# A feed-forward network moved from behind top-k attention into it, with transposes gathered before one copy

## The chip, the cores and the metric

The kernel runs on one core of a Trainium2 chip. The core has a matrix engine (TensorE, PE), a vector engine (VectorE, DVE), a scalar engine (ScalarE, ACT), GpSimd (POOL) and a queue that issues transfers (SyncE, SP). Every engine works through its own instructions in the order in which the program lists them; semaphores tie the engines together. The metric is the time of the launch on the device in microseconds. The program is written in a tile framework that orders the instructions of each engine when it is built, by its own estimate of when each can start; so the order on an engine isn't always the order of the source.

## The reference, cut to what matters

```python
# q, k, v: (8 batches, 8 heads, 576 positions, 64), f32
scores = scale * np.matmul(q, k.transpose(0, 1, 3, 2))        # 576 x 576 for each head
kth = np.partition(scores, -32, axis=-1)[..., -32:-31]        # the 32nd largest of each row
scores = np.where(scores >= kth, scores, -1e9)                # keep the top 32
attn = np.exp(scores - scores.max(-1, keepdims=True))
attn = attn / (attn.sum(-1, keepdims=True) + 1e-09)
x = np.matmul(attn, v)                                        # then heads side by side:
x = x.transpose(0, 2, 1, 3).reshape(4608, 512)                # 4608 tokens of 512
h = np.maximum(x @ w_in, 0.0)                                 # 512 -> 2048
out = (h * h) @ w_out                                         # 2048 -> 512
```

There are two stages: attention with a top-32 selection in every row, for 64 pairs of batch and head, and then a feed-forward network (FFN) over all 4608 tokens. A token's input to the FFN gathers all eight heads of its batch. So a token can go through the FFN once the eight heads of its own batch are done; it needn't wait for the other batches.

## The kernel before

A head's 576 queries are taken in five tiles: four of 128 rows and one of 64. The top 32 of a row are found by VectorE in four rounds: the eight largest values (`max`), and then their replacement by a very small number (`match_replace`).

```python
    psum_pool = tc.alloc_tile_pool(name="apsum", bufs=2, space=bass.MemoryType.PSUM)
    ...
    def _load_transpose(b, h):            # q, k, v of a head; q and k transposed by TensorE
        ...
        nc.vector.tensor_copy(v_sb[:, :, :], v_sb32[:, :, :])             # L81
        nc.vector.tensor_copy(v_sb2[:, :], v_sb232[:, :])                 # L82
        for c in range(nSK_hi):                                           # four chunks
            tps = psum_pool.tile([128, 128], f32, tag="tps")
            nc.tensor.transpose(tps[:64, :128], q_raw[:128, c, :], id128f[:128, :128])
            nc.scalar.activation(qT[:64, c*128:(c+1)*128], tps[:64, :128], Copy)   # L88
            ...                                                           # the same for k, L91
        ...                                                               # the last 64 of q, k

    def _scores(qT, kT, sq0, ql):
        p0 = psum_pool.tile([128, 512], f32, tag="p0", bufs=1)
        nc.tensor.matmul(out=p0[:ql, :512], lhsT=qT[...], rhs=kT[:64, :512])       # L103
        nc.scalar.activation(scores[:ql, :512], p0[:ql, :512], Copy, scale=scale)  # L104
        p0b = psum_pool.tile([128, 64], f32, tag="p0b", bufs=1)
        ...                                                               # columns 512 to 575

    def _softmax(scores, ql):
        ...                                          # 4 rounds of max and match_replace
        nc.vector.tensor_sub(diff[:ql, :], scores[:ql, :], sc_copy[:ql, :])        # L125
        nc.scalar.activation(attnf[:ql, :], diff[:ql, :], Exp,                     # L128
                             bias=bias_t[:ql, :], accum_out=ssum[:ql, :])
        nc.vector.reciprocal(rsum[:ql, :], ssum[:ql, :])                           # L131
        nc.scalar.activation(attn[:ql, :], attnf[:ql, :], Copy, scale=rsum[:ql, :])

    def _ov(attn, v_sb, v_sb2, b, h, sq0, ql):       # attn transposed, times v
        ov_ps = psum_pool.tile([64, 128], f32, tag="ov")
        for c in range(nSK_hi):
            attnT_ps = psum_pool.tile([128, 128], bf16, tag="attnT")
            attnT_sb = work_pool.tile([128, 128], bf16, tag="attnT_sb")
            nc.tensor.transpose(attnT_ps[:128, :ql], attn[:ql, c*128:(c+1)*128], ...)   # L141
            nc.scalar.activation(attnT_sb[:128, :ql], attnT_ps[:128, :ql], Copy)        # L143
            nc.tensor.matmul(out=ov_ps[:64, :ql], lhsT=v_sb[:128, c, :],                # L144
                             rhs=attnT_sb[:128, :ql], start=(c == 0), stop=False)
        ...                                          # the last 64 columns, L148 to L150
        nc.scalar.activation(ov_sb[:64, :ql], ov_ps[:64, :ql], Copy)                    # L153
        nc.sync.dma_start(out=x_dram[h*64:(h+1)*64, b*S+sq0:b*S+sq0+ql], in_=ov_sb[:64, :ql])

    for b in range(B):
        for h in range(H):
            ...                                      # the five tiles of a head
    # pools of attention released; only then the FFN's pools, weights and loop:
    nc.sync.dma_start(out=w_in_sb32[:, :, :], in_=...)          # 4 MB each, f32
    nc.sync.dma_start(out=w_out_sb32[:, :, :], in_=...)
    nc.vector.tensor_copy(w_in_sb[:, :, :], w_in_sb32[:, :, :])           # L184
    nc.vector.tensor_copy(w_out_sb[:, :, :], w_out_sb32[:, :, :])         # L185
    for mi in range(nMT):                            # nine groups of 512 tokens
        nc.sync.dma_start(out=xT[:, :, :], in_=x_re[:, :, m0:m0+MT])
        for dc in range(nDFF):                       # 16 blocks of the inner width
            for kh in range(KH):                     # 4 matmuls
                nc.tensor.matmul(out=hp[:, :], ...)                       # L203
            nc.scalar.activation(rl[:, :], hp[:, :], Relu)                # L206
            nc.vector.tensor_mul(h2[:, dc, :], rl[:, :], rl[:, :])        # L207
        for mt in range(MT // 128):                  # 4 outputs of 16 matmuls
            ...                                                           # L211
            nc.vector.tensor_copy(osb[:, :], op[:, :])                    # L214
            nc.sync.dma_start(out=out[...], in_=osb[:, :])
```

The attention stage uses eight PSUM banks: two each for `tps`, `attnT` and `ov`, one each for `p0` and `p0b`.

Of the kernel before, what the change touches and what calls it, by code (L numbers as in the profile page):

```python
# [15 lines left out]
def kernel(  # L16
# [49 lines left out]
    def _load_transpose(b, h):  # L66
# [18 lines left out]
        for c in range(nSK_hi):  # L85
            tps = psum_pool.tile([128, 128], f32, tag="tps")
            nc.tensor.transpose(tps[:64, :128], q_raw[:128, c, :], id128f[:128, :128])  # L87
            nc.scalar.activation(qT[:64, c*128:(c+1)*128], tps[:64, :128], Copy)  # L88
            tps = psum_pool.tile([128, 128], f32, tag="tps")
            nc.tensor.transpose(tps[:64, :128], k_raw[:128, c, :], id128f[:128, :128])  # L90
            nc.scalar.activation(kT[:64, c*128:(c+1)*128], tps[:64, :128], Copy)  # L91
        tps = psum_pool.tile([128, 128], f32, tag="tps")
        nc.tensor.transpose(tps[:64, :64], q_raw2[:64, :], id128f[:64, :64])
        nc.scalar.activation(qT[:64, 512:576], tps[:64, :64], Copy)
        tps = psum_pool.tile([128, 128], f32, tag="tps")
        nc.tensor.transpose(tps[:64, :64], k_raw2[:64, :], id128f[:64, :64])
        nc.scalar.activation(kT[:64, 512:576], tps[:64, :64], Copy)
        return qT, kT, v_sb, v_sb2

    def _scores(qT, kT, sq0, ql):  # L100
# [4 lines left out]
        p0b = psum_pool.tile([128, 64], f32, tag="p0b", bufs=1)  # L105
# [30 lines left out]
    def _ov(attn, v_sb, v_sb2, b, h, sq0, ql):  # L136
        ov_ps = psum_pool.tile([64, 128], f32, tag="ov")
        for c in range(nSK_hi):
            attnT_ps = psum_pool.tile([128, 128], bf16, tag="attnT")
            attnT_sb = work_pool.tile([128, 128], bf16, tag="attnT_sb")  # L140
            nc.tensor.transpose(attnT_ps[:128, :ql], attn[:ql, c*128:(c+1)*128],  # L141
                                id128[:ql, :ql])
            nc.scalar.activation(attnT_sb[:128, :ql], attnT_ps[:128, :ql], Copy)  # L143
            nc.tensor.matmul(out=ov_ps[:64, :ql], lhsT=v_sb[:128, c, :],  # L144
                             rhs=attnT_sb[:128, :ql], start=(c == 0), stop=False)
        attnT_ps = psum_pool.tile([128, 128], bf16, tag="attnT")
        attnT_sb = work_pool.tile([128, 128], bf16, tag="attnT_sb")
        nc.tensor.transpose(attnT_ps[:64, :ql], attn[:ql, 512:576], id128[:ql, :ql])  # L148
        nc.scalar.activation(attnT_sb[:64, :ql], attnT_ps[:64, :ql], Copy)  # L149
        nc.tensor.matmul(out=ov_ps[:64, :ql], lhsT=v_sb2[:64, :],  # L150
                         rhs=attnT_sb[:64, :ql], start=False, stop=True)
# [4 lines left out]

    for b in range(B):
        for h in range(H):
            qT, kT, v_sb, v_sb2 = _load_transpose(b, h)
            for (sq0, ql) in qtiles:  # L160
                scores = _scores(qT, kT, sq0, ql)
                attn = _softmax(scores, ql)
                _ov(attn, v_sb, v_sb2, b, h, sq0, ql)

    out_pool.release()
# [5 lines left out]

    KH = d_model // 128
    KHO = d_ff // 128
    DFFC = 128
    nDFF = d_ff // DFFC

    wpool = ctx.enter_context(tc.tile_pool(name="wpool", bufs=1))
    w_in_sb32 = wpool.tile([128, KH, d_ff], f32)
    w_out_sb32 = wpool.tile([128, KHO, d_model], f32)
    nc.sync.dma_start(out=w_in_sb32[:, :, :], in_=moe_w_in.rearrange("(kh p) n -> p kh n", p=128))  # L180
    nc.sync.dma_start(out=w_out_sb32[:, :, :], in_=moe_w_out.rearrange("(kh p) n -> p kh n", p=128))
    w_in_sb = wpool.tile([128, KH, d_ff], bf16)
    w_out_sb = wpool.tile([128, KHO, d_model], bf16)
# [62 lines left out]
```

## Time and profile before

| what | value |
|---|---|
| time, median of 4 runs | 2520.69 us (2519.59 to 2521.15) |
| span of the profiled execution | 2517.8 us |
| TensorE clock granted | 1.00 throughout |
| `max` and `match_replace`, 1280 of each | 0.74 to 0.75 us each |
| copies of `attnT` (ACT, 128 columns) | 1024, 0.276 us each |
| copies of `scores` (ACT, 512 columns) | 320, 0.578 us each |
| Relu of 512 columns (ACT) | 144, 0.597 us each |
| squaring of 512 columns (DVE) | 144, 0.692 us each |
| transfers | 57.24 MB, 23 GB/s on average |

A profile shows one execution. Busy time is the time in which an engine works on an instruction; records of neighbouring instructions on one engine overlap a little, so a group's mean times its count is more than the time it takes. In the lists of waits a line names an engine and what it waited to do, what released it, the sum in us, how often, and the longest. In a timeline a line has the start and the duration in us, the engine (PEld is a weight load of TensorE, SPq a transfer's issue), the source line, the operation and its output and input; in brackets stand the idle time before it and what ended that.

### The profile page before, as it was taken

To read this page: it belongs to the slowest core of one execution; us is meant where nothing else is said; L and a number is where in the kernel's file an instruction comes from. 1 tells how busy PE (TensorE), PEld (TensorE's weight loads), DVE (VectorE), ACT (ScalarE), POOL (GpSimd) and SP (SyncE) were. 2 spreads that over 40 slices of the span, in tenths; PEclk is the share of its full clock that TensorE was granted. 3 is DMA by queue.
4 is the path that set the end of the run, shared out by engine and by line. 5 is a ranking of instruction groups with operands and counts; after the bars stand their busy time and mean duration, and the time that the engine had idled before them with its cause. 6 is when DMAs were issued, how large, how long until landed. Compare 5 with 4: busy or idle time off the path is not lost.

```text
span 2517.8 us, 25279 instructions
## 1 busy us (share of the span) xinstructions
PE 1875.3 (74%) x6272; PEld 832.8 (33%) x6272; DVE 2227.2 (88%) x5110; ACT 1362.9 (54%) x4305; POOL 1.1 (0%) x8
## 2 busy tenths in 40 slices
PE   6777777777777777777777777777777777649999
PEld 3333333333333333333333333333333333314444
DVE  7999999999999999999999999999999999965544
ACT  4555555555555555555555555555555555533333
POOL 0000000000000000000000000000000000000000
PEclk9999999999999999999999999999999999999999
DMA  1000100001000000000000000000000000031111
GB/s 37 16 15 17 25 13 16 15 17 25 12 17 15 17 17 12 16 15 17 17 12 17 15 17 17 14 15 16 15 17 15 15 16 10 3 135 51 53 65 42
DMA packets 155011, 57.24 MB, mean 23 GB/s; under 512 B 143088, under 2 KB 147696, under 8 KB 154352
## 3 DMA queue, kind: packets, MB, share of 16 engines
q1 hardware_dynamic: 154864, 55.62, 8.5%
q8 instruction: 50, 0.82, 0.1%
q14 instruction: 97, 0.79, 0.1%
HBM read 41.42 MB, written 14.16 MB: 22 GB/s over the span
## 4 chain that ended last, share of the span: by engine, by line
DVE 64%; PE 26%; ACT 7%; issue 2%; DMA 1%; SPq 0%; DVEq 0%; ACTq 0%
DVE sc_copy L118 23%; DVE max L117 20%; DVE sc_copy L114 7%; DVE max L113 7%; PE p L103 5%; DVE diff L125 5%; PE op L211 5%; PE hp L203 5%; ACT attnf L128 4%; PE tps L90 2%; PE ov_ps L144 2%; PE attnT_ps L141 2%; PE tps L87 2%; ACT scores L104 1%; DVE rsum L131 1%
## 5 line engine op out<-in xcount | busy, mean ns | idle before, releaser
L103 PE MATMUL p<-kT,qT 64*128 64x512 f32 (+1 forms) x640 | 655.9, 1127 | 508.9 <-ACT scores L104 508.9
L118 DVE MATCH_REPLACE8 sc_copy<-max,sc_copy 128x576 f32<-128x576 f32 (+1 forms) x960 | 713.3, 743 | 0.0
L117 DVE MAX8 max<-sc_copy 128x8 f32<-128x576 f32 (+1 forms) x960 | 711.8, 753 | 0.3
L143 ACT ACTIVATE attnT_sb<-attnT_ps 128x128 bf16<-128x128 bf16 (+1 forms) x1280 | 306.7, 265 | 612.2 <-PE attnT_ps L141 603.2
L144 PE MATMUL ov_ps<-attnT_sb,v_sb 128*64 128x128 bf16 (+1 forms) x1280 | 359.8, 286 | 21.9 <-ACT attnT_sb L143 4.2
L103 PEld LDWEIGHTS p<-kT,qT 64*128 64x128 f32 (+1 forms) x640 | 145.8, 287 | 638.9 <-ACT scores L104 638.0
L128 ACT ACTIVATE attnf<-diff,bias_t 128x576 f32<-128x576 f32 (+1 forms) x320 | 246.8, 771 | 125.0 <-DVE diff L125 125.0
L141 PE MATMUL attnT_ps<-id,attn 128*128 128x128 bf16 (+1 forms) x1280 | 297.9, 283 | 8.8 <-ACT attn L133 8.8
L133 ACT ACTIVATE attn<-attnf,rsum 128x576 bf16<-128x576 f32 (+1 forms) x320 | 248.2, 776 | 29.9 <-DVE rsum L131 13.5
L141 PEld LDWEIGHTS <-attn 128*128 128x128 bf16 (+1 forms) x1280 | 118.2, 110 | 367.6 <-issue 156.0
L125 DVE TENSOR_TENSOR diff<-scores,sc_copy 128x576 f32<-128x576 f32 (+1 forms) x320 | 239.6, 749 | 0.0
L113 DVE MAX8 max<-scores 128x8 f32<-128x576 f32 (+1 forms) x320 | 237.6, 742 | 1.6 <-ACT scores L107 1.5
L114 DVE MATCH_REPLACE8 sc_copy<-max,scores 128x576 f32<-128x576 f32 (+1 forms) x320 | 237.6, 743 | 0.0
L106 PEld LDWEIGHTS p0b<-kT,qT 64*128 64x128 f32 (+1 forms) x640 | 169.6, 300 | 173.4 <-issue 138.3
L144 PEld LDWEIGHTS <-v_sb 128*64 128x64 bf16 x1280 | 171.8, 138 | 144.9 <-issue 58.0
L106 PE MATMUL p0b<-kT,qT 64*128 64x64 f32 (+1 forms) x640 | 190.2, 399 | 0.0
L104 ACT ACTIVATE scores<-p 128x512 f32<-128x512 f32 (+1 forms) x320 | 185.1, 578 | 3.3 <-PE p L103 3.3
L206 ACT ACTIVATE rl<-hp 128x512 f32<-128x512 f32 x144 | 86.0, 597 | 174.2 <-PE hp L203 169.4
L131 DVE RECIPROCAL rsum<-ssum 128x1 f32<-128x1 f32 (+1 forms) x320 | 48.6, 152 | 123.9 <-ACT attnf L128 123.9
L203 PE MATMUL hp<-xT,w_in_sb 128*128 128x512 bf16 x576 | 128.1, 384 | 20.2 <-DVE w_in_sb L184 20.2
L150 PE MATMUL ov_ps<-attnT_sb,v_sb 64*64 64x128 bf16 (+1 forms) x320 | 83.1, 260 | 62.5 <-ACT attnT_sb L149 51.6
L207 DVE TENSOR_TENSOR h<-rl 128x512 bf16<-128x512 f32 x144 | 99.5, 692 | 33.1 <-ACT rl L206 33.0
(39 smaller groups left out, 1445.8 us busy)
## 6 DMA issues: line engine op xcount, KB each, us to landing
out_dram<-osb SPq DMA_DIRECT2D x36, 256.0 KB, 2.0
q_raw<-in_q_dram SPq DMA_DIRECT2D x64, 128.0 KB, 2.2
k_raw<-in_k_dram SPq DMA_DIRECT2D x64, 128.0 KB, 2.4
v_sb<-in_v_dram SPq DMA_DIRECT2D x64, 128.0 KB, 2.2
xT<-attn_x SPq DMA_DIRECT2D x9, 512.0 KB, 3.8
attn_x<-ov_sb SPq DMA_DIRECT2D x256, 16.0 KB, 1.7
w_in_sb<-in_moe_w_in_dram SPq DMA_DIRECT2D x1, 4096.0 KB, 12.7
w_out_sb<-in_moe_w_out_dram SPq DMA_DIRECT2D x1, 4096.0 KB, 23.3
```

What stands on the lines that cost most here:

```text
L103: nc.tensor.matmul(out=p0[:ql, :512], lhsT=qT[:64, sq0:sq0+ql], rhs=kT[:64, :512])
L106: nc.tensor.matmul(out=p0b[:ql, :64], lhsT=qT[:64, sq0:sq0+ql], rhs=kT[:64, 512:576])
L113: nc.vector.max(out=max8[:ql, :], in_=scores[:ql, :])
L114: nc.vector.match_replace(out=sc_copy[:ql, :], in_to_replace=max8[:ql, :], in_values=scores[:ql, :], imm_value=NEG)
L117: nc.vector.max(out=max8[:ql, :], in_=sc_copy[:ql, :])
L118: nc.vector.match_replace(out=sc_copy[:ql, :], in_to_replace=max8[:ql, :], in_values=sc_copy[:ql, :], imm_value=NEG)
L125: nc.vector.tensor_sub(diff[:ql, :], scores[:ql, :], sc_copy[:ql, :])
L128: nc.scalar.activation(attnf[:ql, :], diff[:ql, :], Exp, bias=bias_t[:ql, :], accum_out=ssum[:ql, :])
L141: nc.tensor.transpose(attnT_ps[:128, :ql], attn[:ql, c*128:(c+1)*128], id128[:ql, :ql])
L143: nc.scalar.activation(attnT_sb[:128, :ql], attnT_ps[:128, :ql], Copy)
L144: nc.tensor.matmul(out=ov_ps[:64, :ql], lhsT=v_sb[:128, c, :], rhs=attnT_sb[:128, :ql], start=(c == 0), stop=False)
L203: nc.tensor.matmul(out=hp[:, :], lhsT=w_in_sb[:, kh, dc*DFFC:(dc+1)*DFFC], rhs=xT[:, kh, :], start=(kh == 0), stop=(kh == KH - 1))
```

## The change

The change has two parts. First, transposes are gathered: TensorE writes the transposed chunks side by side into one PSUM bank, and ScalarE copies them out at once instead of one by one. That is done for q and k (four chunks of a head) and for the attention weights (four chunks of a tile; the fifth chunk, of 64 rows, has its own copy). `p0b` shares the two banks of `tps`, and `ov` has one bank instead of two. This leaves two of the eight banks for the FFN.

Second, the FFN becomes a generator that is advanced one piece after each attention tile: the load of a group of tokens, then 16 pieces of four matmuls with Relu and squaring, then a piece of 16 matmuls for each 128 tokens of output. A group is handed out once the batches that hold its tokens have been emitted; groups have 512 tokens, or 128 where fewer are left. The weights are loaded before the third head. What is left after the last batch is done at the end. It is meant to give the engines FFN work while attention runs.

```diff
-        for c in range(nSK_hi):
-            tps = psum_pool.tile([128, 128], f32, tag="tps")
-            nc.tensor.transpose(tps[:64, :128], q_raw[:128, c, :], id128f[:128, :128])
-            nc.scalar.activation(qT[:64, c*128:(c+1)*128], tps[:64, :128], Copy)
-            ...                                                    (k alike, then the last 64)
+        for raw, raw2, dst in ((q_raw, q_raw2, qT), (k_raw, k_raw2, kT)):
+            tps = psum_pool.tile([128, 512], f32, tag="tps")
+            for c in range(nSK_hi):
+                nc.tensor.transpose(tps[:64, c*128:(c+1)*128], raw[:128, c, :], id128f[:128, :128])
+            nc.scalar.activation(dst[:64, :512], tps[:64, :512], Copy)
+            tps = psum_pool.tile([128, 512], f32, tag="tps")
+            nc.tensor.transpose(tps[:64, :64], raw2[:64, :], id128f[:64, :64])
+            nc.scalar.activation(dst[:64, 512:576], tps[:64, :64], Copy)
 ...
-        p0b = psum_pool.tile([128, 64], f32, tag="p0b", bufs=1)
+        p0b = psum_pool.tile([128, 512], f32, tag="tps")
 ...
-        ov_ps = psum_pool.tile([64, 128], f32, tag="ov")
+        ov_ps = psum_pool.tile([64, 128], f32, tag="ov", bufs=1)
+        attnT_ps = psum_pool.tile([128, 5, 128], bf16, tag="attnT")
+        attnT_sb = work_pool.tile([128, 5, 128], bf16, tag="attnT_sb")
         for c in range(nSK_hi):
-            ...                                      (transpose, copy and matmul for each chunk)
+            nc.tensor.transpose(attnT_ps[:128, c, :ql], attn[:ql, c*128:(c+1)*128], id128[:ql, :ql])
+        nc.tensor.transpose(attnT_ps[:64, 4, :ql], attn[:ql, 512:576], id128[:ql, :ql])
+        nc.scalar.activation(attnT_sb[:128, :4, :ql], attnT_ps[:128, :4, :ql], Copy)
+        nc.scalar.activation(attnT_sb[:64, 4, :ql], attnT_ps[:64, 4, :ql], Copy)
+        for c in range(nSK_hi):
+            nc.tensor.matmul(out=ov_ps[:64, :ql], lhsT=v_sb[:128, c, :],
+                             rhs=attnT_sb[:128, c, :ql], start=(c == 0), stop=False)
 ...
+    def _ffn(m0, mt):
+        xT = xpool.tile([128, KH, 512], bf16, tag="xT")
+        nc.sync.dma_start(out=xT[:, :, :mt], in_=x_re[:, :, m0:m0+mt])
+        yield
+        h2 = hpool.tile([128, nDFF, 512], bf16, tag="h2")
+        for dc in range(nDFF):
+            hp = psum_pool.tile([128, 512], f32, tag="ffn", bufs=2)
+            ...                                      (4 matmuls, Relu, squaring, of mt columns)
+            yield
+        for done in range(0, mt, 128):
+            op = psum_pool.tile([128, 512], f32, tag="ffn", bufs=2)
+            ...                                      (16 matmuls, copy, store)
+            yield
 ...
     for b in range(B):
         for h in range(H):
+            if b == 0 and h == 2:
+                ...                                  (the loads and casts of w_in and w_out)
             qT, kT, v_sb, v_sb2 = _load_transpose(b, h)
             for (sq0, ql) in qtiles:
                 scores = _scores(qT, kT, sq0, ql)
                 attn = _softmax(scores, ql)
                 _ov(attn, v_sb, v_sb2, b, h, sq0, ql)
-
+                n_tile += 1
+                if n_tile % 40 != 2:
+                    _piece()                         (advance the FFN by one piece)
+        while given + 128 <= (b + 1) * S:
+            mt = 512 if given + 512 <= (b + 1) * S else 128
+            ready.append(_ffn(given, mt))
+            given += mt
+    while ready:
+        _piece()
-    ...                                              (the FFN's own stage behind attention)
```

## The prediction

> **What bounds the kernel now.** I read the page's busy shares first, then the busy times by stretch, then the waits of VectorE, then the timeline of one head boundary, and last the groups of instructions for durations.
>
> ```profile
> PE 1875.3 (74%) x6272; PEld 832.8 (33%) x6272; DVE 2227.2 (88%) x5110; ACT 1362.9 (54%) x4305; POOL 1.1 (0%) x8
> ```
>
> VectorE (DVE) leads with 88%, but the average mixes two stages. The next view cuts the span at 2240.3 us, where the last attention matmul starts, and at 2260.7 us, where the first FFN matmul starts (columns: stretch, length, busy us and count of each engine, clock, DMA share, GB/s).
>
> ```profile
> 0.00:2240.30 2240.30, 1623.97 (x5120) 719.60 (x5120) 2094.09 (x4928) 1276.63 (x4160) 1.09 (x8) 1.00 0.07 16
> 2240.30:2260.70 20.40, 0.17 (x1) 0.00 (x0) 4.43 (x1) 0.22 (x1) 0.00 (x0) 1.00 0.85 326
> 2260.70:2517.80 257.10, 251.16 (x1152) 113.16 (x1152) 128.70 (x181) 86.04 (x144) 0.00 (x0) 1.00 0.17 59
> ```
>
> So: 2240 us of attention, bound by VectorE (2094 busy, 93%), with TensorE at 72%; 20 us in which the chip only fetches weights; 257 us of FFN, bound by TensorE (251 busy) with VectorE half idle. The limits differ, and the second stage's 277 us are serial behind the first. What VectorE waits for:
>
> ```profile
> DVE rsum L131 <- ACT attnf L128: 123.9, 65, 2.0
> DVE w_in_sb L184 <- DMA w_in_sb<-in_moe_w_in_dram: 18.9, 1, 18.9
> DVE v_sb L81 <- DMA v_sb<-in_v_dram: 8.4, 2, 5.5
> ```
>
> In attention it waits once per head, 65 times, 1.9 us each, for Exp. Why Exp is late is in the timeline of a boundary:
>
> ```profile
> 1005.59 0.75 DVE L125 TENSOR_TENSOR diff<-scores,sc_copy 128x576 f32<-128x576 f32 x1
> ...
> 1008.60 0.27 ACT L91 ACTIVATE kT<-tps 64x128 f32<-64x128 f32 x1
> 1008.85 0.22 ACT L94 ACTIVATE qT<-tps 64x64 f32<-64x64 f32 x1
> ...
> 1008.97 0.76 ACT L128 ACTIVATE attnf<-diff,bias_t 128x576 f32<-128x576 f32 x1
> ...
> 1009.86 0.16 DVE L131 RECIPROCAL rsum<-ssum 128x1 f32<-128x1 f32 x1 [1.99 <-ACT attnf L128]
> ```
>
> Exp's input was ready at 1006.34, and Exp starts at 1008.97: ScalarE (ACT) works in order and stands in a ping-pong of ten small q/k copies with as many transposes, with the attnT copies between them.
>
> **What the Trainium skill says.** "Perfetto Trace Analysis", section Optimization Strategy: where the most contended engine changes over time, interleave the regimes. That is this case, by the second fence. The same page, Optimizing Scalar/DVE Operations: every ScalarE and VectorE operation carries a fixed overhead, of which the record shows about twice what holds the engine, since the write's acknowledgement overlaps with the next operation; grouping into larger operations helps. The trace agrees on the overlap: 0.66 us after the start of a 749 ns subtraction the next operation starts, so 0.09 us are hidden. "ScalarE: Activation LUTs", What ACT_TABLE_LOAD costs, gives 0.833 ns per element; here 64 columns take 223 ns and 128 take 276, 0.83 per element. "TensorE: Matmul & The Clock Gate", Back-to-back issue gap, has about 216 ns for a warm 512-column matmul; the trace has 64 in 13.98 us, 218 ns.
>
> **The change, part by part.**
>
> *Merged copies.* Per head, ten q/k copies (8 x 0.270 + 0.219 + 0.213 = 2.59 us) become four: the 64x512 f32 evacuation takes 0.578 (scores row), so 2 x 0.578 + 2 x 0.216 = 1.59. Saved 1.0 x 64 = 64 us of ScalarE. Per query tile, 4 x 0.276 + 0.269 = 1.37 becomes one copy of 512 columns, estimated at 0.276 + 384 x 0.00083 = 0.595, plus 0.269 = 0.86; saved 0.51 x 320 = 163. None of this is on the bound, but the ping-pong goes.
>
> *Does the 124 us wait go?* I follow one tile in the compiled instruction order of the changed kernel, where Exp(i) starts at 0, with durations from the steady tiles: scores evacuation 0.77, the f32 score matmul 1.40 to 3.4, the five attnT transposes at 0.11 us pace to 4.2, their copies to 5.0, the five output matmuls to 5.7, their copy, and Exp(i+1) can start near 5.9. VectorE asks for it every 2094 / 320 = 6.54 us. It also leaves two 0.66 us operations between the subtraction and the reciprocal, where Exp and its accumulator read need 0.97, so Exp may be 0.35 late for nothing. Ordinary tiles don't stall. With an FFN group of 4 x 0.218 = 0.87 us ahead of the output matmuls the chain takes 6.4, but the tile then has a further 0.6 us VectorE operation: 7.15. At head boundaries there are two orders. In 26 of them (mostly without FFN work beside) the q/k copies are spread over the preceding tile and Exp comes in time. In 37 of them q64, k512, k64 stand ahead of Exp: the chain becomes about 7.6 without and 8.2 with FFN work, where 6.54 + 0.35 and 7.15 + 0.35 + 0.6 are free. That makes 0 to 0.7 us; I take 0.3 x 37 = 11 us. So of 124 us some 110 go.
>
> *Weights early.* The two loads are issued near 8 us, behind the inputs of two heads; they landed 12.7 and 23.3 us after issue in the kernel before, so by 21 and 32. The casts stand in VectorE's order near 23 and 38 us. The 20.4 us go; 8.85 us of casts enter VectorE's stage.
>
> *FFN inside attention.* 4608 tokens become 8 groups of 512 and 4 of 128. All but the last 512 and the last 128 run beside the next batch. They bring to VectorE 7 x 16 = 112 squarings of 512 columns (0.692 alone, 0.60 back to back: 67 us), 48 of 128 columns (estimated 0.692 - 384 x 0.00104 = 0.29, so 0.20: 10 us), 31 output copies (0.60: 19 us), and the casts: 105 us. TensorE gets about 7/8 of 251, some 225 us, so about 1850 in 2240: near 83%, not the bound. The output groups of 16 matmuls (3.5 us) are laid in the compiled order around the output matmuls of a tile; counted as above they end at about 8.4, just before the score matmul that can start at 7.15 + 1.40 = 8.55, and a score block is made almost a tile ahead.
>
> *Batch starts.* In the order, the first relu of a batch stands ahead of the second Exp after the last needed store (store 1.7, load 3.8, four matmuls, relu): about 1.4 us late, 7 times: 10 us.
>
> *Tail.* After the last reciprocal only the last 512 and 128 tokens are left: the fourth tile's store lands and the load of 512 tokens arrives at about +5.5; 16 groups at 0.88 = 14.1; 4 output groups of 16 x 0.218 = 13.9; 16 groups for 128 tokens with two PSUM buffers and relu behind each, estimated 0.5 each = 8; one output group 3.5, copy 0.7, store 2.4, and 0.8 of latencies: 49 us.
>
> *Sum.* VectorE in attention 2094 + 105 inserted + 9 at the start + 9 of small unlisted gaps (2237.3 at the last reciprocal, less 2094 and 134 of listed waits) + 11 + 10 + 1.4 at the last tile = 2239; + 49 tail = 2288; + 3 from span to measured time (2520.7 against 2517.8) = 2291. I say 2295, since what I can have missed is nearly all on the long side.
>
> **The rivals.**
> 1. *The Exp wait stays or moves to every tile.* For it: the boundary chain still has ACT, PE, ACT in turn, and the margin in ordinary tiles is only 0.6 + 0.35 us; FFN matmuls and relus enter both queues in order. Against it: the chain above, and ScalarE falls to about half busy. A stall of 1.9 us per head would give 2295 + 110 = about 2405; 0.3 us on each of 320 tiles about 2390.
> 2. *TensorE becomes the bound in tiles with an output group.* For it: 5.1 us of attention matmul (1624 / 320) plus 3.5 is above 7.15. Against it: busy time counts latency, and score blocks are made ahead. At 2 us for each of 31 groups: 2355.
> 3. *The FFN is hidden entirely and attention stalls vanish.* Then VectorE's work alone counts: about 2270.
> 4. *The FFN stands still while a load is awaited, and VectorE with it,* because queues are in order: each batch would pay a round trip of some 6 us, 7 times: 2330.
>
> **Range and chances.** Rivals 2 to 4 give 2270 to 2355, and rival 1 in full is unlikely, so 2265 to 2350 should hold it 8 times in 10. To miss 2% (2470) nearly all that is hidden would have to come back: chances 94 in 100 faster, 5 within 2%, 1 slower.
>
> **What would show it.** In the changed profile: VectorE busy near 2230 us and above 95%; its wait of reciprocal for Exp below 40 us in all; no long stretch without TensorE before the FFN; ScalarE near 1145 us; last reciprocal near 2240 us; a tail of 45 to 55 us with TensorE full. Wrong would be: a new wait of VectorE for relu (squaring) or for an output group above 30 us; a wait of scores for the score matmul on most tiles; a tail over 60 us.

## The result, and the profile after

| what | before | after |
|---|---|---|
| time, median | 2520.23 us (2519.59 to 2522.05, 13 runs) | 2341.05 us (2337.70 to 2342.45, 8 runs) |
| ratio, with its 95% interval | 1 | 0.9285 (0.9276 to 0.9294) |
| start of the last reciprocal of the attention | 2237.2 us | 2292.0 us |
| from there to the end of the span | 280.6 us | 47.3 us |

The change saves 179 us. The prediction said 2295 us, with 2265 to 2350 as its range; the time is 46 us above the point. The FFN's stage behind the attention is gone as foreseen (280.6 us became 47.3), but the attention grew by 55 us where almost nothing was expected.

The profile after, in the same order as before. The page's busy times, and its TensorE clock in forty slices:

```profile
PE 1758.6 (75%) x6464; PEld 797.6 (34%) x6464; DVE 2199.4 (94%) x5158; ACT 1158.6 (50%) x3009; POOL 1.1 (0%) x8
...
PEclk9999966555566565665656655566555655657558
```

VectorE is at 94% of the span; above 95% was foretold. The busy times by stretch, cut at the last reciprocal (columns as before):

```profile
0.00:2292.20 2292.20, 1720.04 (x6246) 778.40 (x6246) 2180.72 (x5121) 1143.48 (x2973) 1.09 (x8) 0.63 0.09 24
2292.20:2339.30 47.10, 38.60 (x218) 19.17 (x218) 18.67 (x37) 15.12 (x36) 0.00 (x0) 0.92 0.13 43
```

VectorE works 2181 of the first 2292 us, so about 111 us of it are idle. Its list of waits names nearly all of them:

```profile
DVE rsum L126 <- ACT attnf L123: 81.1, 80, 2.4
DVE h L179 <- ACT rl L178: 20.1, 31, 7.1
DVE osb L187 <- PE op L184: 13.3, 5, 2.9
DVE max L108 <- ACT scores L102: 8.5, 21, 0.5
DVE v_sb L81 <- DMA v_sb<-in_v_dram: 8.4, 2, 5.5
```

The wait for the weights is gone. The waits for output groups (`osb`) and 12 of the 20 us for Relu lie in the tail. What remains is the wait of the reciprocal for Exp: 81 us, where the prediction had 12. It is the old wait of 124 us, by the same pair of instructions. All but some 1 us after the last tile lies in batches 1 to 7, 10 to 13 us in each; batch 0, which has no FFN work beside it, has none. And it lies at head boundaries, that is where the next head's q and k are transposed during a head's later tiles. The timeline of one boundary shows why Exp is late:

```profile
799.20 0.47 PE L101 MATMUL p0b<-kT,qT 64*64 64x64 f32 x2
...
807.57 0.59 ACT L89 ACTIVATE qT<-tps 64x512 f32<-64x512 f32 x1
...
808.61 0.31 PE L91 MATMUL tps<-id128f,q_raw 64*64 64x64 f32 x1
...
808.72 0.75 DVE L120 TENSOR_TENSOR diff<-scores,sc_copy 128x576 f32<-128x576 f32 x1
808.96 0.22 ACT L92 ACTIVATE qT<-tps 64x64 f32<-64x64 f32 x1
...
809.23 1.06 PE L88 MATMUL tps<-id128f,k_raw 128*64 128x128 f32 x4 [0.31 <-ACT qT L92]
...
810.33 0.59 ACT L89 ACTIVATE kT<-tps 64x512 f32<-64x512 f32 x1 [1.15 <-PE tps L88]
...
810.97 0.31 PE L91 MATMUL tps<-id128f,k_raw 64*64 64x64 f32 x1 [0.68 <-ACT kT L89]
...
811.32 0.22 ACT L92 ACTIVATE kT<-tps 64x64 f32<-64x64 f32 x1 [0.40 <-PE tps L91]
811.44 0.77 ACT L123 ACTIVATE attnf<-diff,bias_t 128x576 f32<-128x576 f32 x1
...
812.33 0.16 DVE L126 RECIPROCAL rsum<-ssum 128x1 f32<-128x1 f32 x1 [1.27 <-ACT attnf L123]
...
812.68 0.21 ACT L102 ACTIVATE scores<-p0b 64x64 f32<-64x64 f32 x1
```

Exp's input is ready near 809.5, but Exp starts at 811.44. Between them ScalarE, which works in order, waits for k's transposes, and these wait for a bank: the transposes of k start at 809.23, released by the copy of q's last 64 columns, and k's last 64 wait in turn for the copy of its first 512. There are two `tps` banks, but the other one holds `p0b` of the current head's fifth tile since 799.20 (q and k are the next head's), and the copy that frees it (812.68) stands behind Exp. So q64, k512 and k64 take turns in one bank.

The second thing to read is TensorE's pace, here at the first FFN work (start and duration in us):

```profile
278.80 2.07 PE L98 MATMUL p<-kT,qT 64*128 64x512 f32 x2 [0.61 <-ACT scores L99]
...
292.40 3.59 PE L175 MATMUL hp<-xT,w_in_sb 128*128 128x512 bf16 x8
295.92 1.12 PE L98 MATMUL p<-kT,qT 64*128 64x512 f32 x2
```

The same pair of score matmuls takes 2.07 us in one line and 1.12 in the other, 17 us later. The eight FFN matmuls took 3.59 us, 0.449 each; the prediction had 0.218, from a stage in which TensorE ran without a break. So in attention the array mostly runs at half rate, and the clock row agrees from the sixth slice on.

### The profile page after: what moved, and what is told of

It reads as the page before. It is cut to its first block, busy times and chain, and to the rows that moved or that the text cites. A ratio compares the mean times of both kernels' runs of the same rounds, so it can differ in the third digit from the quotient of the medians.

```text
span 2339.3 us, 23300 instructions
## 1 busy us (share of the span) xinstructions
PE 1758.6 (75%) x6464; PEld 797.6 (34%) x6464; DVE 2199.4 (94%) x5158; ACT 1158.6 (50%) x3009; POOL 1.1 (0%) x8
## 4 chain that ended last, share of the span: by engine, by line
DVE 54%; PE 31%; ACT 12%; DMA 2%; issue 2%; SPq 0%
DVE sc_copy L113 18%; DVE max L112 16%; PE p L98 10%; DVE sc_copy L109 6%; DVE max L108 5%; ACT attnf L123 5%; PE hp L175 5%; DVE diff L120 5%; PE tps L88 3%; PE ov_ps L142 3%; PE op L184 3%; PE attnT_ps L136 2%; ACT scores L99 2%; PE p0b L101 2%; DVE h L179 1%
## 5 line engine op out<-in xcount | busy, mean ns | idle before, releaser
L98 PE MATMUL p<-kT,qT 64*128 64x512 f32 (+1 forms) x640 | 609.6, 1051 | 379.6 <-ACT scores L99 379.1
L139 ACT ACTIVATE attnT_sb<-attnT_ps 128x512 bf16<-128x512 bf16 (+1 forms) x320 | 177.5, 555 | 573.1 <-PE attnT_ps L138 572.7
L175 PE MATMUL hp<-xT,w_in_sb 128*128 128x512 bf16 (+1 forms) x768 | 260.0, 459 | 21.0 <-DMA xT<-attn_x 11.2
L147 ACT ACTIVATE ov_sb<-ov_ps 64x128 bf16<-64x128 f32 (+1 forms) x320 | 83.5, 261 | 281.0 <-PE ov_ps L144 280.5
L142 PE MATMUL ov_ps<-attnT_sb,v_sb 128*64 128x128 bf16 (+1 forms) x1280 | 176.2, 286 | 55.5 <-ACT attnT_sb L139 52.8
L136 PE MATMUL attnT_ps<-id,attn 128*128 128x128 bf16 (+1 forms) x1280 | 174.9, 285 | 43.4 <-ACT attn L128 43.2
L101 PEld LDWEIGHTS p0b<-kT,qT 64*128 64x128 f32 (+1 forms) x640 | 146.5, 275 | 158.8 <-ACT attn L128 65.4
L184 PE MATMUL op<-w_out_sb,h 128*128 128x512 bf16 x576 | 180.7, 457 | 21.3 <-DVE h L179 21.1
L142 PEld LDWEIGHTS <-v_sb 128*64 128x64 bf16 x1280 | 125.0, 150 | 177.4 <-issue 156.0
L126 DVE RECIPROCAL rsum<-ssum 128x1 f32<-128x1 f32 (+1 forms) x320 | 50.1, 157 | 81.9 <-ACT attnf L123 81.1
L179 DVE TENSOR_TENSOR h<-rl 128x512 bf16<-128x512 f32 (+1 forms) x192 | 105.8, 554 | 20.1 <-ACT rl L178 20.1
```

Of the source, the lines that this page charges most:

```text
L98: nc.tensor.matmul(out=p0[:ql, :512], lhsT=qT[:64, sq0:sq0+ql], rhs=kT[:64, :512])
L101: nc.tensor.matmul(out=p0b[:ql, :64], lhsT=qT[:64, sq0:sq0+ql], rhs=kT[:64, 512:576])
L136: nc.tensor.transpose(attnT_ps[:128, c, :ql], attn[:ql, c*128:(c+1)*128], id128[:ql, :ql])
L175: nc.tensor.matmul(out=hp[:, :mt], lhsT=w_in_sb[:, kh, dc*DFFC:(dc+1)*DFFC], rhs=xT[:, kh, :mt], start=(kh == 0), stop=(kh == KH - 1))
L184: nc.tensor.matmul(out=op[:, :], lhsT=h2[:, kh, done:done+128], rhs=w_out_sb[:, kh, :], start=(kh == 0), stop=(kh == KHO - 1))
```

## The experiments

Two theories for the 81 us, and both can hold:

- **A, the bank:** `p0b` in the `tps` banks makes q's and k's transposes take turns ahead of Exp.
- **B, the rate:** an FFN group in the attention stage holds TensorE about 1.8 us (4 x 0.449), not 0.87, and so delays what Exp and the scores wait for.

All runs below were timed beside the kernel before, which took 2520 us each time.

### Each theory by itself: e1_own_bank and e2_quarter

e1 gives `p0b` a bank of its own, taken from `attnT`:

```diff
-        p0b = psum_pool.tile([128, 512], f32, tag="tps")
+        p0b = psum_pool.tile([128, 64], f32, tag="p0b", bufs=1)
-        attnT_ps = psum_pool.tile([128, 5, 128], bf16, tag="attnT")
+        attnT_ps = psum_pool.tile([128, 5, 128], bf16, tag="attnT", bufs=1)
```

> The changed kernel, but p0b has a bank of its own again and attnT has one bank in place of two (eight banks as before). In the changed kernel VectorE waits 81 us for Exp, all at head boundaries. Theory A (bank): these come from p0b sharing the two banks of tps: the next tile's p0b holds one bank until its copy, which stands behind Exp, so q64, k512 and k64 take turns in the other bank, transpose and copy one after the other, ahead of Exp. Then the wait falls below 35 us and the time to 2285 to 2305 us. Theory B (rate): they come from FFN matmuls that run at about half the rate that I reckoned with (0.45 to 0.5 us each in place of 0.218) and stand among the boundary's transposes. Then the wait stays above 60 us and the time above 2320 us.

e2 leaves out three of the four products of each `hp` block and twelve of the sixteen of each output; its output isn't the FFN's:

```diff
-            for kh in range(KH):                     # 4
+            for kh in range(1):
-            for kh in range(KHO):                    # 16
+            for kh in range(4):
```

> The changed kernel with a quarter of the FFN's matmuls: one of the four of each hp group and four of the sixteen of each output group; the rest of the products is left out, and all copies, Relus, squarings, loads and stores stay. Theory A (bank): the wait of VectorE for Exp stays above 55 us, and the time falls only by what the tail's matmuls took (some 25 us of 47) plus a little, to about 2305 us. Theory B (rate): the wait falls below 35 us, and the time to about 2265 us.

| run | time | ratio | wait of the reciprocal for Exp | last reciprocal |
|---|---|---|---|---|
| after | 2341.05 us | 0.9285 (0.9276 to 0.9294) | 81.1 us, 80 times | 2292.0 us |
| e1_own_bank | 2299.11 us | 0.9120 (0.9107 to 0.9134) | 55.8 us, 64 times | 2251.1 us |
| e2_quarter | 2293.66 us | 0.9099 (0.9084 to 0.9115) | 56.8 us, 63 times | 2258.5 us |

Each takes a third of the wait away, and neither takes it all. e1 gains 42 us. Only 25 of them are the wait for Exp; VectorE also waits 6 us less for Relu and 5 less for scores in the attention, and works 4 less. e2 gains 47, of which 14 are in the tail, where fewer matmuls are left (33.7 instead of 47.3 us). The same boundary in the timeline of e1:

```profile
774.46 1.06 PE L88 MATMUL tps<-id128f,q_raw 128*64 128x128 f32 x4
...
804.93 0.59 ACT L89 ACTIVATE qT<-tps 64x512 f32<-64x512 f32 x1 [1.33 <-PE p0b L101]
...
806.02 1.06 PE L88 MATMUL tps<-id128f,k_raw 128*64 128x128 f32 x4
...
807.12 0.59 ACT L89 ACTIVATE kT<-tps 64x512 f32<-64x512 f32 x1 [0.43 <-PE tps L88]
...
807.77 0.75 DVE L120 TENSOR_TENSOR diff<-scores,sc_copy 128x576 f32<-128x576 f32 x1
...
808.55 0.78 ACT L123 ACTIVATE attnf<-diff,bias_t 128x576 f32<-128x576 f32 x1 [0.17 <-DVE diff L120]
...
810.03 0.15 DVE L126 RECIPROCAL rsum<-ssum 128x1 f32<-128x1 f32 x1
```

Here k's four large transposes are done before the subtraction starts, Exp is released by the subtraction itself, and the reciprocal has no wait. So taking turns in one bank is gone where it was read. But the framework also changed its order: it now transposes q a head ahead (774.46, copied at 804.93), so q's transposes no longer stand at this boundary. How much of the 25 us comes from the bank itself and how much from this order isn't separated. Nor is the single bank of `attnT` free: batch 0, without a wait in the changed kernel, has 4.9 us in e1.

### Both together: e5_own_quarter

The edits of e1 and e2 in one kernel; it too leaves three quarters of the FFN's products out.

> Both edits at once: p0b in a bank of its own, and a quarter of the FFN's matmuls (the rest of the products is left out). Each alone left some 56 us of the 81 us of waits for Exp. If bank and rate are two separate causes at the same boundaries, the wait falls to 35 us or less and the time to about 2260 us (2292 less some 30). If they are one cause seen from two sides, or if the four copies ahead of Exp are a third that neither edit touches, it stays between 45 and 57 us and the time above 2275 us.

It took 2240.86 us, ratio 0.8891 (0.8878 to 0.8904). The line of its list of waits:

```profile
DVE rsum L126 <- ACT attnf L123: 18.6, 21, 1.1
```

The wait goes from 81.1 to 18.6 us: 62 less, where the single edits took 25 and 24. So neither edit does the other's work, and together they take three quarters of the wait, more than the sum of the two alone. The last reciprocal comes at 2205.5 us, 86.5 earlier (41 and 33.5 for the single edits). What e2 and e5 show of B is that the time of the FFN's matmuls counts; they don't show what it would bring to run them at full rate: the score matmuls kept their slow pace in both (1.13 us each in the mean).

### The two parts of the change alone: e3_merge_only and e4_interleave_only

e3 has the merged copies with the FFN behind the attention as before; e4 has the FFN inside, with the small copies of before:

```diff
 # e3: the FFN's stage of before; transposes, copies and banks of after
+    for b in range(B):
+        for h in range(H):
+            ...                                  (five tiles of a head, no piece of the FFN)
+    ...                                          (weights and FFN behind it, as before)
 # e4: after, with
+            tps = psum_pool.tile([128, 128], f32, tag="tps")
+            nc.scalar.activation(qT[:64, c*128:(c+1)*128], tps[:64, :128], Copy)   # each chunk
+            nc.scalar.activation(attnT_sb[:128, :ql], attnT_ps[:128, :ql], Copy)   # each chunk
```

> Only the first part of the change: gathered transposes and their banks, with the FFN as its own stage behind attention as before. The 124 us of waits for Exp should nearly go, since in the compiled order every head has its q and k copies spread over the tile before: 2520 less 110 to 124 is 2396 to 2410 us. Both theories say so, because no FFN matmul is in attention and the order avoids the turn-taking. A time above 2450 us would speak against the reading that the ping-pong of small copies made Exp late.

> Only the second part: the FFN interleaved as in the changed kernel, but q, k and attnT copied chunk by chunk as before (p0b shares the banks of tps, ov has one bank, so that two are left for the FFN). The wait for Exp should be at least the 124 us of before. Theory A and B alike: 2341 + 45 to 2341 + 90, so 2385 to 2430 us, and a sum of both parts' gains (with e3) near or above the gain of the whole.

| run | time | ratio | wait for Exp | last reciprocal | tail |
|---|---|---|---|---|---|
| e3_merge_only | 2397.69 us | 0.9513 (0.9499 to 0.9527) | 3.7 us, 3 times | 2114.4 us | 281.5 us |
| e4_interleave_only | 2468.23 us | 0.9796 (0.9772 to 0.9819) | 196.4 us, 131 times | 2417.8 us | 47.6 us |

The merged copies alone bring 123 us, and they remove the old wait but for 3.7 us, with the same shared bank. So the shared bank costs next to nothing in an attention stage without FFN work. It can't be told from this run whether the FFN's work itself or the framework's order makes the difference: in e3 the next head's four q and k copies stand between the third and the fourth tile's Exp in 62 of the 64 heads, a tile later than at the boundary shown above. The interleaving alone brings 52 us, not the 90 to 135 of the expectation: the wait for Exp rose from 124 to 196 us, and a wait for scores of 20 us came with it. The two gains add up to 175 us of the whole's 179. The tail in e4 is as short as in the changed kernel, so this was lost inside attention.

From e3 to the changed kernel one reads where the interleaving's gain went: the tail shrinks by 234 us (281.5 to 47.3), and the attention grows by 178 (2114.4 to 2292.0): 57 us remain. Of the 178, 77 are the wait for Exp (81.1 less 3.7); most of the rest is the work that VectorE took over, measured below.

### Is it the rate: d1_fill and d2_fill_tied

To make TensorE fast in attention, eight matmuls whose result nobody uses were put after each tile. In d1 they read a constant; in d2 the tile's own attention weights:

```diff
-        attnT_ps = psum_pool.tile([128, 5, 128], bf16, tag="attnT")
+        attnT_ps = psum_pool.tile([128, 5, 128], bf16, tag="attnT", bufs=1)
+    def _fill():                                   # d2: _fill(attn, ql), rhs=attn[:ql, :512]
+        fill_ps = psum_pool.tile([128, 512], f32, tag="fill_ps", bufs=1)
+        for _i in range(8):
+            nc.tensor.matmul(out=fill_ps[:, :], lhsT=id128[:, :], rhs=fill_sb[:, :])
```

> A test of the rate by itself: the changed kernel with attnT in one bank and eight matmuls of 512 columns after every tile that nothing reads, in the bank that this frees (p0b stays in tps). Theory: TensorE runs attention at half its rate because it isn't busy without a break, and filling it brings the full rate. Then the pair of score matmuls takes about 1.1 us in place of 2.07, the pace within FFN groups is 0.22 us in place of 0.45, and the filler is nearly free: wait for Exp 50 to 85 us, time 2310 to 2350 us. Rival: the rate is limited by something else, such as a limit on power. Then the pair stays at 2.07 us, the filler costs 8 x 0.43 = 3.4 us of TensorE in each tile, TensorE becomes the bound, and the time rises above 2600 us.

> As the kernel with filler before, but each tile's eight filling matmuls read that tile's attention weights, so that they can't be done in advance; in the first filler run they were laid in bursts of 20 and were used up at half time. Theory: the filler keeps TensorE busy all through; the score pair takes 1.1 us nearly everywhere, and the wait for Exp is 30 to 70 us: 2290 to 2335 us. Rival: eight a tile leave gaps in which the rate falls back, so the pair's mean stays above 1.6 us, the filler costs time on TensorE, and the time is above 2345 us.

d1 took 2402.45 us, 0.9532 (0.9518 to 0.9546): 61 us slower than the changed kernel, and far from the 2310 to 2350 expected. The framework's order used all its fillers up by 1130 us, in bursts of up to some twenty, so the run holds both cases. Busy times by stretch, with and without fillers:

```profile
20.00:1130.00 1110.00, 1081.05 (x5256) 471.64 (x5355) 1009.45 (x2358) 520.70 (x1369) 0.00 (x0) 1.00 0.09 24
1200.00:2350.00 1150.00, 871.77 (x3186) 394.32 (x3222) 1092.33 (x2578) 572.66 (x1500) 0.00 (x0) 0.58 0.08 20
```

And two lines of its timeline in the filled half:

```profile
599.85 5.14 PE L201 MATMUL fill_ps<-fill_sb,id 128*128 128x512 bf16 x20
604.92 1.12 PE L98 MATMUL p<-kT,qT 64*128 64x512 f32 x2
```

With fillers TensorE is busy 97% of the time and at full rate (1.12 us for the pair, 0.26 per filler); without them it is 76% busy and mostly at half rate. That part of B is shown: the half rate goes with TensorE's own pauses. But the wait for Exp was 140 us, some 23 in each batch of the filled half against 10 to 15 in the other. Batch 0, which has no FFN work and had no wait in the changed kernel, now has 24 us; e1, with the same single bank for `attnT`, has 4.9 there. So the fillers, which stand in the same queue as the work that Exp needs, cost more than the faster clock gave.

d2 took 2349.17 us, 0.9324 (0.9309 to 0.9340), with a mean clock of 0.841 (0.637 in the changed kernel), and its wait for Exp was 89.8 us. The score matmuls became shorter, 754 ns in the mean instead of 1051, and it took 8 us more than the changed kernel. So what a full rate would save by itself isn't settled: any filler adds work where the rate is to be tested, and both runs have one bank for `attnT` instead of two.

### Less work for VectorE: v1_gpsimd

With e1's bank VectorE is busy 95% of the span, so its own work is next. v1 is e1 with the squarings and the casts of v and of the weights on GpSimd:

```diff
-            nc.vector.tensor_mul(h2[:, dc, :mt], rl[:, :mt], rl[:, :mt])
+            nc.gpsimd.tensor_mul(h2[:, dc, :mt], rl[:, :mt], rl[:, :mt])
-        nc.vector.tensor_copy(v_sb[:, :, :], v_sb32[:, :, :])          # and v_sb2, w_in, w_out
+        nc.gpsimd.tensor_copy(v_sb[:, :, :], v_sb32[:, :, :])
```

> The kernel with p0b in its own bank, and the squarings and the casts of v and of the weights moved from VectorE to the idle GpSimd. If VectorE's busy time is the bound, its work falls by 112 x 0.60 + 48 x 0.20 + 64 x (0.20 + 0.10) + 9 = about 105 us, of which waits give back a part: 2299 less 60 to 105 is 2195 to 2240 us. If instead the chain through TensorE and ScalarE is now nearly as long as VectorE's tile, the waits for Exp grow by more than half of that and the time stays above 2250 us.

It took 2217.33 us (2216.66 to 2217.93), ratio 0.8797 (0.8782 to 0.8811). VectorE's busy time fell by 88.5 us against e1 (2195.2 to 2106.7), and the time by 82. GpSimd's groups show what the work costs there (busy us, mean ns, then its idle time):

```profile
L179 POOL TENSOR_TENSOR h<-rl 128x512 bf16<-128x512 f32 x128 | 137.4, 1090 | 149.1 <-ACT rl L178 148.3
...
L81 POOL CAST v_sb<-v_sb 128x256 bf16<-128x256 f32 x64 | 25.7, 402 | 1751.5 <-issue 1693.6 <-PE ov_ps L142 51.2 <-DMA v_sb<-in_v_dram 6.7
```

A squaring takes 1.09 us instead of the 0.69 it took on VectorE, and this matters little: GpSimd is busy 222 of 2216 us. Outputs wait for `h2` in the tail, which is 2 us longer than in e1 (50.2 against 48.1).

Two things came with the move. First, VectorE can be slower beside GpSimd: a subtraction, 0.74 us in the median and in e1 never above 0.9, took 5.92 while GpSimd cast a weight for 7.62.

```profile
20.56 7.62 POOL L208 CAST w_in_sb<-w_in_sb 128x8192 bf16<-128x8192 f32 x1 [10.93 <-DMA w_in_sb<-in_moe_w_in_dram]
...
22.86 5.92 DVE L120 TENSOR_TENSOR diff<-scores,sc_copy 128x576 f32<-128x576 f32 x1
```

Second, the framework's order changed. In the changed kernel and in e1 a head beside FFN work has about five of the sixteen Relus of a group; in v1 one head has all sixteen, and it is the same in v3 and v5. The FFN's matmuls then come in longer rows and mostly at the full rate, here 0.23 us each:

```profile
294.57 2.81 PE L175 MATMUL hp<-xT,w_in_sb 128*128 128x512 bf16 x12
```

The wait for Exp fell from 55.8 to 38.3 us with it, and lies in the first one or two heads of a batch; at the other boundaries none exceeds 0.3 us. So the 82 us aren't the lighter VectorE alone: up to the last reciprocal it works 73 us less (2176.5 to 2103.2), and the rest comes from waits. How much the new order contributes isn't separated.

### Spreading the next head's transposes: v2, v3 and v5

In the changed kernel there was no wait, with one exception, at the 26 boundaries where most of the next head's q and k copies come after the third tile's Exp (19 of them without FFN work beside). v2 writes such a spread into e1: loads after the first tile, q's transposes after the second, k's after the third. v3 adds the squarings and weight casts on GpSimd; v5 also the casts of v.

```diff
+                if following is not None:
+                    if ti == 0:
+                        nxt = _load(*following)                  # with the casts of v
+                    elif ti == 1:
+                        _transpose(nxt[0], nxt[1], nxt[4])       # q
+                    elif ti == 2:
+                        _transpose(nxt[2], nxt[3], nxt[5])       # k
```

> The kernel with p0b in its own bank, with the loads of the next head after the first tile of a head, its q transposes after the second and its k transposes after the third. If the copies ahead of Exp at the boundary are what is left of the wait (56 us), they should be further from it in the order, and the wait should fall below 40 us and the time to 2265 to 2285 us. If the FFN matmuls in between are what is left, little changes: 2290 to 2305 us.

> Both edits that helped a wait: p0b in its own bank, loads and transposes of the next head spread over a head's tiles, and squarings and casts on GpSimd. The spread kernel lost what it gained because the cast of v stood in VectorE's order before its buffer was free (37 us of waits); on GpSimd that wait stops nobody. From 2217 us (38 us of waits for Exp) less some 25: 2180 to 2200 us. If the waits move to the score copies or to the output copies, 2205 to 2220 us.

> The run v3_spread_gps was meant to have the casts of v on GpSimd, but its edit left them on VectorE; here they are on GpSimd, and nothing else is changed against it. If the loss of both spread kernels is the cast of v standing in VectorE's in-order queue ahead of the release of its buffer, then that wait (41.1 us in v3_spread_gps) and the casts' own busy time on VectorE (64 times about 0.7 us, 45 us) both leave VectorE: 2307 less some 85 is 2220 us, between 2190 and 2235, and no new wait over 20 us on VectorE. Whether it beats v1_gpsimd (2217) is open: it depends on whether the wait for Exp stays at the 44 us of v3_spread_gps or returns to the 8.6 us of v2_spread. Rival: the late v only moves to TensorE (the output matmuls then wait for v, and Exp and the score matmuls behind them): then the wait for Exp or for scores rises by 30 us or more, and the time stays above 2250.

| run | time | ratio | wait for Exp | VectorE busy |
|---|---|---|---|---|
| v2_spread | 2310.80 us | 0.9165 (0.9151 to 0.9179) | 8.6 us | 2210.3 us |
| v3_spread_gps | 2307.21 us | 0.9160 (0.9146 to 0.9173) | 44.1 us | 2149.7 us |
| v5_spread_gps_v | 2216.50 us | 0.8792 (0.8780 to 0.8804) | 34.5 us | 2114.6 us |

v2 did what it was made for, and was 12 us slower than e1. Its list of waits gives one reason:

```profile
DVE v_sb L81 <- PE ov_ps L143: 37.0, 51, 1.4
...
DVE rsum L127 <- ACT attnf L124: 8.6, 8, 1.1
```

A new wait of 37 us took the place of most of the 47 that went. The rest is VectorE's busy time, 15 us more than in e1 (2210.3 against 2195.2), though it has the same instructions; what lengthened it stays open. The cast of v now stands in VectorE's order before its buffer is free; an output matmul of an earlier head still reads it. v3 was expected at 2180 to 2200 with the casts of v on GpSimd, but its edit left them on VectorE, so it couldn't show that; the wait stayed, at 41.1 us. v5 mends this, and the wait is gone. The time falls by 91 us, to 2216.5, as that expectation had it (2220): 41 of wait, 35 of VectorE's busy time and 10 less of waiting for Exp account for 86. But v5 and v1 can't be told apart (2213.93 to 2220.05 and 2216.66 to 2217.93). Once the bank is free and VectorE has less to do, the spread adds nothing; in both runs most boundaries have no FFN work beside them.

### Too much moved: v4_diff_gps

v3 with the subtraction ahead of Exp on GpSimd:

```diff
-        nc.vector.tensor_sub(diff[:ql, :], scores[:ql, :], sc_copy[:ql, :])
+        nc.gpsimd.tensor_sub(diff[:ql, :], scores[:ql, :], sc_copy[:ql, :])
```

> The kernel before this in the list, with the subtraction ahead of Exp (0.66 us of VectorE in each of 320 tiles, 211 us) on GpSimd, where a squaring of 512 columns took 0.87 us. VectorE's tile falls from about 6.5 to 5.9 us, which is the length that I reckoned for the chain from Exp to Exp over TensorE. If VectorE stays the bound: 2190 less 150 to 211, 1980 to 2040 us. If the chain takes over: 2060 to 2150 us, with waits of VectorE for Exp or for scores above 100 us.

It took 2395.96 us, 0.9506 (0.9492 to 0.9520). One line of its groups and one of its waits:

```profile
L121 POOL TENSOR_TENSOR diff<-scores,sc_copy 128x576 f32<-128x576 f32 x256 | 359.9, 1406 | 1262.1 <-DVE bias_t L117 1233.4 <-ACT kT L91 17.9 <-DVE v_sb L82 8.2
```

```profile
DVE rsum L127 <- ACT attnf L124: 329.2, 305, 5.4
```

The 0.87 us for a squaring in the expectation was a mean over squarings of 512 and of 128 columns; one of 512 takes 1.09. VectorE lost 188 us of work (2149.7 to 1961.8) and gained 285 us of waiting for Exp, 1.08 us at nearly every tile. The subtraction takes 1.41 us on GpSimd and 0.75 on VectorE, and it is the step that Exp waits for. So this step's length counts fully, and a squaring's doesn't. The Trainium skill, "GPSIMD Engine Reference", section Engine selection, advises against GpSimd for elementwise work with two inputs, as about twice slower; the subtraction agrees (1.9 times). What the slower engine costs depends on who waits: this step cost 89 us against v3, the squarings of v1 next to nothing.

## Why the prediction was right in its range and 46 us short

By its own steps:

- **The limit and its move: right.** VectorE stayed the bound, the weights' 20 us went without a wait of VectorE for them, the separate stage went, and the tail is 47.3 us (predicted 49). From span to time there are 1.8 us (predicted 3).
- **ScalarE: right.** 1158.6 us busy against 1145 predicted.
- **VectorE's inserted work: right; its other work shrank.** It works 2180.7 us up to the last reciprocal, 86.6 more than before (2094.1) and not 105. Counted in the trace from each instruction's start to the next one's (or to its own end, if that is earlier), the inserted operations take 109 us: 80 for squarings, 20 for output copies, 9 for casts. The work that was there before takes 22 less, 16 of it in `max` (874 to 858); the prediction has nothing of it, and why it is so stays open. The start (8.8 against 9) fits, and small gaps took 4 instead of 9.
- **TensorE: not the bound, as said, but by two errors that cancel.** It is busy 1720 us in the attention, where 1850 was said. The merged copies alone lower it from 1622 to 1406 us (e3), which wasn't reckoned with, and the FFN work then adds some 315, not 225 (7/8 of 251 would be 220): its matmuls take about 0.449 us there and not 0.218.
- **Batch starts: right.** VectorE's wait for Relu in attention was 7.9 us; 10 were said.
- **Ordinary tiles don't stall: right.** The rival of a stall at every tile is false, and so is that of output groups as the bound: tiles with an output group have waits of about 1 us at most, and only at head boundaries. A wait for scores of 9 us was missing from the sum. But the waits reach further into a head than one tile, see below.
- **Head boundaries: this is the step that failed.** "That makes 0 to 0.7 us; I take 0.3 x 37 = 11 us" measured 81.1 us (with the 1.1 of the last tile).

The sum closes: Exp +69 (81.1 against 11 and 1.4), scores +9, Relu -2, VectorE's work -18, gaps -5, together +53: the last reciprocal at 2292 and not 2239. That the error stayed at 46 us is in part luck: three terms were set 25 us too high together, which offset a third of the 78 by which the other two were too low.

In the failed term the mechanism was right, and so was the number of heads. In 37 heads at least the next head's q512, q64 and k512 stand ahead of the third tile's Exp, much as the prediction had it, and 36 of them hold a wait of over 0.3 us. Of the 26 other boundaries one does, but the 19 without FFN work are among them. Three sizes in it were wrong:

1. **How many tiles.** I followed one tile for each boundary. There were 76 waits over 0.3 us in 37 heads, so two for each, mostly in a head's second to fourth tiles, and one more after the last tile.
2. **How much is free.** For boundaries with FFN work I let the chain take 7.15 + 0.35 + 0.6. But 7.15 already holds the 0.6 of the squaring. With 7.50 free and 8.2 needed each wait is 0.7; without FFN work it was 7.6 against 6.89, 0.7 too. 77 waits of 0.7 would have been 54 us. And even 7.50 was too much: in the 46 waiting tiles with a squaring, VectorE's own time from one reciprocal to the next, without the wait, is 7.07 us in the mean. The chain was sized well: from one Exp to the next there are 8.36 us in these tiles (8.09 over all waiting tiles, 6.80 elsewhere).
3. **TensorE's rate.** The four FFN matmuls were put at 4 x 0.218 = 0.87 us, and take 4 x 0.449 = 1.8. Since the chain as a whole was nearly as long as reckoned, something else in it must have been sized too long; which part stays open. The measured wait is 81.1 / 77 = 1.05 us.

The experiments confirm what this chain is made of: give `p0b` its own bank (with the order that comes of it) and 25 us of wait go, shorten the FFN matmuls and 24 go, do both and 62 go. The last 18.6 us stay unexplained. How much of the 81 is due to the half rate alone stays open.

Rival 1, the wait that stays, was set at 1.9 us for each head or 0.3 at every tile; measured are 1.3 us per head in the mean (81.1 / 64). The guard in the prediction, "below 40 us in all", was the signal that showed it.

## What to carry to other kernels

Work moved beside another stage runs at that stage's pace, not at its own: take the durations for a prediction from the stage that receives it. When one engine is the bound and others stand in its chain in order, count how many iterations a late step touches, and count each operation's time as slack only once; then look for buffers that two users share, since a small one (64 columns here) can hold a bank across a boundary. An off-path engine may take slow work that nobody waits for (squarings on GpSimd, 82 us gained with the casts and the new order), but not a step of the chain (one subtraction, 89 us lost). And where a framework orders the instructions, read the order again after every edit, however small: e1 and v1 each changed more than their lines say.

## What the runs showed of the hardware that was not expected

- **TensorE at half rate for most of the time, at 75% busy.** The score pair takes 2.07 us or 1.12. The Trainium skill, "TensorE: Matmul & The Clock Gate", section What's actually happening, says that the array is at half clock until it has been busy for a window of some 3.4 us, and falls back after an idle one. On the way up the trace agrees: in the 3.4 us before each of the 37 changes to full rate in the changed kernel TensorE was busy for over 80%, mostly for all of it. On the way down it differs: in the 13.7 us before 36 of the 38 changes to half rate TensorE had no pause of 3.4 us. So the fall here needs no idle window, and 1697 us of the recorded 2045 are at 0.5, though TensorE is busy three quarters of the time.
- **A clock of 1.00 that isn't measured.** The profile's clock shows 1.00 for the attention stage of the kernel before, and for the first 300 us of the changed one, while the score pair takes 2.0 to 2.1 us there. The trace's clock records begin at 295.9 us in the changed kernel, where the score pair first takes 1.12 us; before the first one the row shows full speed. In the kernel before they begin at 2265.2 us, and there the FFN's first matmuls go from 0.43 to 0.22 us apart. So the line "TensorE clock granted 1.00 throughout" of the kernel before is to be read by its durations: 1.13 us for each score matmul in the mean, which is the slow pace. In e2 and e5 the clock shows full speed throughout, with records of the last 16 us alone, and the same matmuls take 1.13 us too.
